# Range checks of a first unit's q, k and v: read again and squared near the end of the program, with a new order of all steps

## The chip, the core and the metric

One core of a Trainium2 chip runs the whole program. The metric is the device time of one execution in microseconds (us); lower is better. The engines are named as in the profile: PE (matmul), PEld (its weight loads), DVE (vector engine), ACT (scalar engine), POOL (GpSimd, which here issues most of the transfers) and SP (which issues the rest).

## What is computed

A gated linear recurrence over 768 positions for 4 batches and 8 heads of width 48, then a two-layer network on its output with squared ReLU:

```python
a_re_n, a_im_n = a_re * scale, a_im * scale   # scale = min(mag, 0.999) / (mag + 1e-6)
for t in range(S):
    S_re, S_im = ar * S_re - ai * S_im + k_t (x) v_t, ar * S_im + ai * S_re
    y[:, :, t] = q_t . S_re
x = y as (3072, 384)
h = x @ w_in                     # w_in (384, 2048), float64
out = maximum(h, 0)**2 @ w_out   # w_out (2048, 384), float64
```

Inputs q, k, v, a_re and a_im are float32.

## The kernel before

`fast_path` cuts the 3072 rows into six **units** of 512 rows (`NU`, numbered 0 to 5). For each unit `load(n)` brings a, q, k and v in, `chain(n)` turns the gates into running products (normalising, a scan over the positions, scaling of q and k), `pairs(n)` computes scores and sums per pair of heads on PE, and `dense(n, grp)` runs the two-layer network on the unit's rows, 256 at a time. The last unit has its own first layer (`whole`, L1922 to L1978) and every second layer from unit 1 on is done with seven products in place of eight (`seven`), its matmuls at L2051 in steps called `half`: eight matmuls each. Before any of that, the float64 weights are fetched in sixteen pieces and put into float32 by `convert`: two ACT operations (L975, L976) and two DVE operations (L978, L981) for each piece.

The fast path holds only for inputs in a certain range, so it also computes **checks**. `squares(j)` (called in `rest`, L1534 for q and k, L1537 for v) squares what a unit has loaded and sums it into `sums`; ACT does it, writing the squares to a scratch tile `junk`. For one unit this is six operations of 128x768. Near the end of the program `inspect(i)` reads each of the sixteen weight pieces a second time (a POOL transfer at L996 into a quarter of the tiles `ff`, of 768 KB), and DVE looks at their bits (`look`, L1001 and L1003). Piece i uses quarter i modulo 4, so the transfer of piece i waits for the look of piece i-4. When every check is done, `collect` (DVE, L2143 to L2156) puts them together, one PE matmul (L2160) adds over the partitions, and DVE (L2162) writes `flag`. Each engine then loads the flag into a register (L882) and branches on it (L2234, L2262): to `general_path`, a slow kernel for any input, or to the last steps of the fast path. These last steps, `plan.ends`, are what is left of the last `seven` after its matmuls are issued and isn't PE's: four DVE additions (L2074) that gather the results into the output tiles `ot`, and three transfers of output rows (L2002).

Two constants set what this change touches. `AFTER` is the number of units whose `squares` isn't run in `rest`, but by `squares_of`, after all `inspect` steps. It is 0 in the kernel before. `squares_of(n, j)` for j = 0, 1, 2 (q, k, v) issues a POOL transfer of the unit's q, k or v (768 KB, in runs of 768 bytes) into one quarter of `ff`, and one ACT operation of 128x1536 that squares it in place and sums into `sums`.

The order of the instructions on each engine is made by a planner (`Plan`). Every piece of work is a **step**, with an engine, a duration, what it reads and writes, and a number from the list `ORDER`, which has one entry for each step in the order in which the code creates them. The planner plays the program through: whenever an engine is free, it takes that one of its ready steps that has the smallest number. In the kernel before, the order that comes out is on every engine the ascending order of the numbers. An engine runs its queue strictly in this order, so a step whose inputs aren't there holds up all that stand behind it on the same engine. Where PE would stand still for long, the planner puts in matmuls on the identity whose result nobody reads (L880, "fill").

Names of steps in the prediction: the first transposes of unit 0's scaled q and k by PE are L1710, their copies out of PSUM by ACT are L1713, the scores are L1732, and the first layer of the network begins at L1850.

Of the kernel before, what the change touches and what calls it, by code (L numbers as in the profile page):

```python
# [767 lines left out]
def fast_path(ctx, tc, q, k, v, a_re, a_im, moe_w_in, moe_w_out, out, flag, ots, blocks_of):  # L768
# [69 lines left out]
    AFTER = 0  # L838
# [255 lines left out]
    def chain(n):  # L1094
# [503 lines left out]
        def rest(*zs):  # L1598
# [6 lines left out]
            for z in zs:  # L1605
                twist(z)
                if n >= AFTER:
                    squares(z)
# [660 lines left out]
```

## Time and profile before

| | us |
|---|---|
| median of 3 runs | 650.94 |
| lowest and highest of them | 650.93, 651.6 |
| the profiled execution, its own time | 652.71 |
| its span, first to last instruction | 651.0 |

The mean clock that PE was granted over the span is 0.997. The span is read as three parts: from the start to about 85 us, where unit 0 is prepared and its scores are computed and where all the fill lies; from there to about 648 us, where PE runs with hardly a gap; and the last 3 us, in which the last results are added and written out.

### The profile page before, as it was taken

How to read it: one execution, taken by the hardware profiler on the slowest of the kernel's cores; microseconds unless marked ns; L12 is line 12 of the kernel's file. 1: busy time of each engine (PE TensorE's matmuls, PEld its weight loads, DVE VectorE, ACT ScalarE, POOL GpSimd, SP SyncE). 2: the span in 40 equal slices, each digit the busy share in tenths (PEclk: the TensorE clock that was granted, in tenths of full speed). 3: DMA queues.
4: the chain of work that ended last, by engine and by line, in shares of the span. 5: the costliest groups of instructions: out<-in, count | busy, mean ns of one | idle time of the engine just before them, and what ended most of it. 6: DMA issues, size and time to landing. Idle time of an engine off the chain costs nothing.

```text
span 651.0 us, 13374 instructions
## 1 busy us (share of the span) xinstructions
PE 641.1 (98%) x5046; PEld 575.9 (88%) x5046; DVE 571.2 (88%) x1187; ACT 382.8 (59%) x652; POOL 152.4 (23%) x258
## 2 busy tenths in 40 slices
PE   8998999999999999999999999999999999999998
PEld 7988987578778988999988998989999989988997
DVE  7999999999799998988997996995979998359993
ACT  7989889956665265368166648156658164145500
POOL 6503455123200022051043051121050030022210
PEclk9998999999999999999999999999999999999999
DMA  7972679237620156352176354165260162257651
GB/s 224 298 255 57 163 213 203 72 89 189 165 82 2 37 126 149 93 143 52 49 161 146 73 131 88 24 152 159 58 171 16 45 143 66 61 202 242 209 184 31
DMA packets 34630, 81.79 MB, mean 126 GB/s; under 512 B 7894, under 2 KB 13411, under 8 KB 34556
## 3 DMA queue, kind: packets, MB, share of 16 engines
q0 software_dynamic: 17024, 58.60, 33.6%
q1 hardware_dynamic: 15356, 20.04, 12.1%
q10 hardware_dynamic: 2176, 2.20, 1.2%
q8 instruction: 42, 0.69, 0.5%
q14 instruction: 32, 0.26, 0.1%
HBM read 48.76 MB, written 4.72 MB: 82 GB/s over the span
## 4 chain that ended last, share of the span: by engine, by line
PE 73%; DVE 12%; ACT 4%; DMA 3%; issue 2%; SPq 0%; POOL 0%; DVEq 0%; ACTq 0%; POOLq 0%
PE d L1850 24%; PE d L2051 24%; PE d L1897 5%; PE sc L1732 5%; PE yp L1790 3%; PE tr L1762 2%; PE d L1943 2%; PE yp L1794 2%; PE tr L1943 2%; DVE f L1243 1%; PE sc L1943 1%; DMA aq<-in_a_im_dram 1%; PE d L1710 1%; DVE g L2065 1%; DVE aq L1228 1%
## 5 line engine op out<-in xcount | busy, mean ns | idle before, releaser
L1850 PE MATMUL d<-xT,w 128*128 128x256 f32 x912 | 203.2, 380 | 0.0
L1850 PEld LDWEIGHTS d<-xT,w 128*128 128x128 f32 x912 | 171.8, 190 | 24.0 <-issue 0.4
L2051 PE MATMUL d<-w,g 128*128 128x192 f32 x576 | 101.0, 327 | 0.0
L2051 PEld LDWEIGHTS d<-w,g 128*128 128x128 f32 x576 | 94.3, 190 | 1.2 <-issue 0.4
L1882 ACT ACTIVATE g<-d 128x512 f32<-128x512 f32 x76 | 45.0, 592 | 81.7 <-PE d L1850 79.0
L2051 PE MATMUL d<-T,g 128*128 128x192 f32 x432 | 77.1, 329 | 0.4 <-DVE g L2065 0.3
L2051 PEld LDWEIGHTS d<-T,g 128*128 128x128 f32 x432 | 70.6, 190 | 2.0 <-DVE g L2065 0.6
L2007 POOL DMA_DIRECT2D out_dram<-ot x22 | 12.5, 569 | 202.3 <-DVE ot L2074 181.3
L1682 ACT COPY QT<-aq 32x512 f32<-32x512 f32 x57 | 35.0, 615 | 39.7 <-DVE aq L1679 27.9
L1639 POOL DMA_DIRECT2D KC<-f x56 | 35.0, 630 | 80.8 <-DVE f L1593 30.3
L2065 DVE TENSOR_TENSOR g<-g 128x512 f32<-128x512 f32 x72 | 48.1, 685 | 4.8 <-PE d L2051 4.0
L1883 ACT ACTIVATE g<-g 128x512 f32<-128x512 f32 x80 | 50.5, 631 | 2.6
L1679 DVE STREAM_TRANSPOSE aq<-f 128x768 f32<-128x768 f32 x40 | 49.0, 1277 | 0.3
L1800 ACT COPY yt<-yp 112x512 f32<-112x512 f32 x24 | 26.5, 1106 | 34.2 <-PE yp L1794 34.2
L880 PEld LDWEIGHTS d<-ident 128*128 128x128 f32 x348 | 42.6, 203 | 3.0 <-POOL ident masks.py:199 1.7
L880 PE MATMUL d<-ident 128*128 128x128 f32 x348 | 43.3, 287 | 1.7 <-POOL ident masks.py:199 1.7
L1593 DVE TENSOR_TENSOR f<-aq 128x768 f32<-128x768 f32 (+1 forms) x56 | 44.0, 838 | 0.5
L1897 PE MATMUL d<-w,g 128*128 128x384 f32 x128 | 43.7, 491 | 0.0
L1732 PE MATMUL sc<-QT 96*64 96x128 f32 (+1 forms) x736 | 41.0, 258 | 1.5 <-ACT QT L1713 0.8
L1732 PEld LDWEIGHTS sc<-QT 96*64 96x64 f32 x736 | 37.1, 140 | 4.6 <-issue 2.3
L1738 DVE TENSOR_TENSOR A<-sc,mask 128x512 f32<-128x512 f32 x45 | 29.8, 681 | 9.2 <-PE sc L1732 9.2
L1897 PEld LDWEIGHTS d<-w,g 128*128 128x128 f32 x128 | 23.7, 190 | 15.0 <-issue 0.4
(276 smaller groups left out, 1167.5 us busy)
## 6 DMA issues: line engine op xcount, KB each, us to landing
QT<-aq SPq DMA_DIRECT2D x152, 64.0 KB
f<-in_moe_w_in_dram POOLq DMA_DIRECT2D x8, 768.0 KB, 6.0
f<-in_moe_w_out_dram POOLq DMA_DIRECT2D x8, 768.0 KB, 5.0
out_dram<-ot POOLq DMA_DIRECT2D x22, 192.0 KB, 2.8
KC<-f POOLq DMA_DIRECT2D x20, 192.0 KB, 4.5
xT<-yt SPq DMA_DIRECT2D x36, 96.0 KB
aq<-in_q_dram POOLq DMA_DIRECT2D x8, 384.0 KB, 5.4
aq<-in_k_dram POOLq DMA_DIRECT2D x8, 384.0 KB, 5.7
```

Source lines behind the costliest of these rows:

```text
L880: plan = Plan(lambda b: pe.matmul(bank[b][:, 0:C], lhsT=ident, rhs=ident, start=True, stop=True), ["d2", "d1", "d0"], lambda ap: tc.nc.val ...
L1593: lambda j=j, r=r, o=o: dve.tensor_tensor(out=o[:, :, :, r * D:(r + 1) * D], in0=qk[:, j], in1=a[:, r], op=ALU.mult), late[z])
L1639: lambda i=i, queue=queue, lo=lo, hi=hi, a0=a0, a1=a1: queue.dma_start(out=kc[lo:hi, i], in_=nat[a0:a1]),
L1679: lambda nat=nat, dst=dst, j=j: dve.transpose(out=dst[:, j], in_=nat), rank)
L1682: lambda b=b, t=t, T6=T6: act.copy(out=t[32 * b:32 * b + 32, b], in_=T6[32 * b:32 * b + 32, i % 2, b]),
L1732: pe.matmul(sa[r:r + C // 2, j, :, lo:32], lhsT=T[:, j, 1, h, ts(late, C // 2)], rhs=T[:, j, 0, h].rearrange("p (c t) -> p c t", c=W)[:, : ...
L1850: pe.matmul(ps, lhsT=w1[:, f // FP, m, ts(f % FP, C)], rhs=xT[:, n % 2, m, ts(grp, G)], start=(m == 0), stop=(m == NM - 1))
L1882: act.activation(out=o, in_=ps, func=AF.Relu)
L1883: act.activation(out=o, in_=o, func=AF.Square)
L1897: pe.matmul(ps, lhsT=gt[:, f % 2, ts(i, C)], rhs=w2[:, f], start=(f == 0), stop=(f == NF - 1))
L2051: pe.matmul(bank[b][:, 0:DH], lhsT=gs(r, h)[:, j - 4 * h], rhs=w(j), start=first and j == 0, stop=last and j == NT - 1)
L2065: step("DVE", tt(4 * C), gk(x0, h) + gk(x1, h), gk(o, h), lambda: dve.tensor_tensor(out=gs(o, h), in0=gs(x0, h), in1=gs(x1, h), op=op), (0 ...
```

## The change

The code differs in one constant, and in the numbers of `ORDER`:

```diff
-    AFTER = 0
+    AFTER = 1
```

With it `rest` leaves out six steps of unit 0, and the program gains six before `verdict`:

```python
if n >= AFTER:
    squares(z)
...
for n in range(AFTER):
    for j in range(3):
        squares_of(n, j)
verdict()
```

The number of steps stays the same (2434), so the old and the new list can be laid beside each other: the entries of the six left out are taken from the old list, and the six added stand ahead of the last three, which are `collect`, the matmul of the verdict and the flag. The last lines of the two lists:

```diff
-5840 5931 5855 5960 5901 6014 5933 6071 5947 6098 5976 6119 6030 6169 6088 6184 6114 6213
-6135 6227 6186 6245 6200 6275 6301 6356 6362
+5897 6013 5938 6058 5959 6072 5999 6126 6030 6163 6074 6180 6089 6220 6143 6237 6179 6264
+6197 6279 6236 6310 6253 6349 6365 6419 6426
```

Nearly every number differs, most of them little. Laid out by engine, the numbers say this of the places that the prediction uses:

| place | old numbers | new numbers |
|---|---|---|
| the six squares of unit 0 (ACT) | 259, 267, 288, 296, 484, 523 | left out |
| q, k and v of unit 0 near the end: transfers (POOL) | none | 6197, 6236, 6253 |
| their squares (ACT) | none | 6279, 6310, 6349 |
| first L1710 of unit 0 (PE) | 542 | 548 |
| one conversion, L975 and L976 (ACT) | 640, 649 | 500, 514 |
| one L1565 of 128x192 and one L1585 of unit 0 (DVE) | 547, 573 | 472, 521 |
| look of the last weight piece (DVE) | 6275 | 6264 |
| look of the piece before it (DVE) | 6245 | 6237 |
| the addition next to that look (DVE, L2074) | 6259 | 6234 |
| the half of eight matmuls that this addition waits for (PE) | 6239 | 6211 |
| PE steps with a number above that half's, without the verdict's | 14 | 17 |
| `collect` (DVE) | 6301 | 6365 |
| the last addition (DVE, L2074) that stands ahead of `collect` in the new order | 6356 | 6359 |
| the half that this addition waits for (PE) | 6317 | 6328 |
| PE steps with a number above that half's, without the verdict's | 8 | 8 |
| the verdict's matmul (PE) | 6356 | 6419 |
| PE steps behind it, eight matmuls each | 6359, 6372, 6385, 6398, 6411, 6424 | 6422, 6435 |
| the flag (DVE) | 6362 | 6426 |

The numbers are used as ranks only: they say what stands ahead of what on an engine.

256 rows, old and new, of the table ORDER are left out of this document.

## The prediction

> **What bounds the kernel now.** I read the page's busy times first, then the windows by stage.
>
> ```profile
> PE 641.1 (98%) x5046; PEld 575.9 (88%) x5046; DVE 571.2 (88%) x1187; ACT 382.8 (59%) x652; POOL 152.4 (23%) x258
> L880 PE MATMUL d<-ident 128*128 128x128 f32 x348 | 43.3, 287 | 1.7 <-POOL ident masks.py:199 1.7
> 28.00:42.00 14.00, 12.44 (x107) 11.77 (x104) 12.45 (x49) 12.06 (x18) 4.44 (x8) 1.00 1.02 324
> 42.00:58.40 16.40, 14.75 (x118) 13.39 (x117) 16.16 (x52) 16.23 (x25) 1.63 (x3) 1.00 0.26 79
> 58.40:84.90 26.50, 26.30 (x433) 24.30 (x433) 25.40 (x58) 20.86 (x31) 11.98 (x20) 0.94 0.60 140
> 84.90:160.00 75.10, 75.10 (x365) 57.28 (x366) 73.39 (x143) 60.65 (x100) 28.43 (x42) 1.00 0.64 153
> 160.00:576.00 416.00, 414.37 (x3445) 378.00 (x3440) 361.33 (x736) 223.92 (x395) 76.74 (x121) 1.00 0.39 96
> ```
>
> The columns of a window are its length, then the busy time of PE, PEld, DVE, ACT and POOL, the clock, the DMA share and GB/s. PE looks full everywhere, but 43.3 us of it is fill (L880), all ahead of 84.9. From 84.9 to 576 PE stands still for 416.00 - 414.37 = 1.6 us. So the program is a front of 85 us, in which PE waits for others, and then a block of PE work that nothing shortens here. The front can be won, or the end.
>
> In the front both DVE and ACT are full. From 42.00 to 58.40 ACT works 16.23 of 16.40 us and DVE 16.16. DVE's idle time from 28.00 to 84.90 is 1.55 + 0.24 + 1.10 = 2.9 us. The chain of waits goes through ACT just before PE's first scores:
>
> ```profile
> 49.13 0.92 ACT junk L1537 x2
> 53.15 0.82 ACT junk L1537 x2
> 53.97 1.84 ACT xT L976
> 56.50 1.91 ACT QT L1713 x4
> 58.46 3.60 PE sc L1732 x32
> 639.81 8.01 PE d L2051 x48
> 647.85 0.35 DVE ot L2074
> ```
>
> Here two of the checks that the change moves (L1537, squares of v) lie on the chain, ahead of the copies (L1713) that PE waits for. At the other end the chain is 48 matmuls and then one DVE addition.
>
> **The change, part one: what goes.** The six squares, by the groups of ACT from 24 to 58.4 us:
>
> ```profile
> L1534 ACT ACTIVATE junk<-aq 128x768 fp8e5<-128x768 f32 x4 | 3.4, 859 | 0.1
> L1537 ACT ACTIVATE junk<-v 128x768 fp8e5<-128x768 f32 x2 | 1.6, 824 | 0.0
> L1534 ACT ACTIVATION_READ_ACCUMULATOR junk<-aq 128x1 f32 x4 | 0.8, 189 | 0.0
> L1537 ACT ACTIVATION_READ_ACCUMULATOR junk<-v 128x1 f32 x2 | 0.4, 187 | 0.0
> L976 ACT ACTIVATE w<-w 128x768 f16<-128x768 int16 x4 | 7.8, 1944 | 0.1
> L975 ACT ACTIVATE w<-w 128x768 uint32<-128x768 uint32 x4 | 3.7, 936 | 0.0
> ```
>
> 3.4 + 1.6 + 0.8 + 0.4 = 6.2 us of ACT go. The new numbers put one conversion, L975 and L976, 0.94 + 1.94 = 2.9 us, ahead of the first copy L1713 in their place, so ACT has 6.2 - 2.9 = 3.3 us less ahead of it. On the chain itself stood 0.92 + 0.82 = 1.7 us.
>
> What is late next is DVE, which loses no instruction. The first transposes (L1710) read what DVE has multiplied, and DVE was without a gap there. The new numbers even put two more DVE operations ahead of them:
>
> ```profile
> 53.18 0.46 DVE L1585 TENSOR_TENSOR aq<-aq,e 128x288 f32<-128x288 f32 x1
> 53.56 0.35 DVE L1565 TENSOR_TENSOR f<-aq,e 128x192 f32<-128x192 f32 x1
> 84.84 1.13 PE L1850 MATMUL d<-xT,w 128*128 128x256 f32 x4
> 58.40:62.00 3.60, 3.54 (x33) 3.21 (x33) 3.60 (x10) 3.57 (x4) 1.58 (x3) 0.53 0.38 86
> ```
>
> That is 0.46 + 0.35 = 0.8 us later for the transposes, if nothing is gained, and 0 if DVE finds as much idle time ahead of them to fill. Both ends are near, and I take the middle: **the front ends 0.4 us later**. The bounds are wider. Below nothing: all of DVE's idle time is closed, -2.9 us. Above: the window from 58.40 shows PE at a clock of 0.53 for 3.6 us, which costs about 0.47 x 3.6 = 1.7 us; a second stretch like it, with the 0.8, makes +2.5 us.
>
> **Part two: what comes.** Three transfers of 768 KB on POOL and three squares of 128x1536 on ACT.
>
> ```profile
> L1114 ACT ACTIVATE f<-aq 128x1536 f32<-128x1536 f32 x10 | 14.9, 1489 | 3.6 <-DMA aq<-in_a_im_dram 3.5
> L1114 ACT ACTIVATION_READ_ACCUMULATOR f<-aq 128x1 f32 x10 | 1.9, 192 | 0.0
> DMA to landing us min/median/max: 4.6/5.4/9.5
> 620.00:651.00 31.00, 27.81 (x172) 27.25 (x170) 19.37 (x46) 1.58 (x3) 2.58 (x4) 1.00 0.29 99
> 628.43 0.56 DVE L1001 TENSOR_SCALAR f<-f 128x768 uint32<-128x768 uint32 x1
> 629.03 0.95 DVE L1003 TENSOR_REDUCE odd<-f 128x1 f32<-128x768 uint32 x1
> ```
>
> A square is 1.49 + 0.19 = 1.7 us. ACT is busy 1.58 of the last 31 us and POOL 2.58, so 5.1 us of squares and three issues cost nothing there: their cover is idle engines. The landing times are those of the same 768 KB at L996. What they could delay is the verdict. Let E be the end of PE's last matmul (647.82 before). A half of eight matmuls takes 8.01 / 6 = 1.335 us. The last of the three transfers needs the quarter of weight piece 14, and that piece's look stands behind an addition that waits for a half with 17 PE steps behind it: E - 22.8. With the addition (0.35) and the look (0.56 + 0.95) that is E - 20.9; landing after 5.4 to 9.5 us E - 15.5 to E - 11.4; squared by E - 9.7 at the latest. `collect` can't start much sooner anyway: the addition ahead of it waits for a half with 8 steps behind it, E - 10.8. So the third square is in time for PE's verdict.
>
> **Part three: where the verdict stands.** In the old order six halves stand behind the verdict's matmul on PE, in the new one two. These rows, from the timeline and, for the register load, from the tile `flag`, price that:
>
> ```profile
> 633.90 0.41 DVE L2143 TENSOR_SCALAR x<-sums 128x12 f32<-128x12 f32 x4
> 635.68 0.16 DVE L2156 TENSOR_REDUCE good<-good 128x1 f32<-128x7 f32 x1
> 639.62 0.19 PE L2160 MATMUL tr<-col,good 128*1 128x1 f32 x2
> 639.85 0.14 DVE L2162 TENSOR_SCALAR flag<-tr 1x1 int32<-1x1 f32 x1 [1.40 <-PE tr L2160]
> 642.65 0.35 DVE L2074 TENSOR_TENSOR ot<-ot,d 128x192 f32<-128x192 f32 x1 [2.65 <-PE d L2051]
> L882 DVEq TENSOR_LOAD <-flag x1: 539/539/539, 642.7 to 642.7; - x1
> 646.47 1.08 DVE L2074 TENSOR_TENSOR ot<-ot,d 128x192 f32<-128x192 f32 x3 [3.47 <-issue]
> 647.85 0.35 DVE L2074 TENSOR_TENSOR ot<-ot,d 128x192 f32<-128x192 f32 x1 [0.30 <-PE d L2051]
> ```
>
> `collect` takes 635.84 - 633.90 = 1.9 us, so it is done by E - 7.8 at the latest. The flag is written 639.99 - 639.62 = 0.37 us after the verdict's matmul starts. DVE loads it at 642.7, and its next operation, the first of the four behind the branch, starts at 646.47: **3.8 us from load to work**, of which "issue" says that it waited for nothing the profile shows. Before, this fitted under PE's last matmuls: three additions ran by 647.55, and the last one waited only for PE. In the new order the verdict's matmul starts at E - 2 x 1.335 - 0.1 = E - 2.8, the flag is there at E - 2.4, DVE goes on at E + 1.4, does three additions (1.08) and starts the last at E + 2.4. It was E + 0.03. The rest, the last transfer out, stays as it was behind that addition. **The end costs 2.4 us.** Bounds: 0, if the 3.8 us shrink to the 0.54 of the load; and +4.4, if the verdict also comes 2 us late.
>
> The Trainium skill, page "Advanced Engine Details and Errata", section "Control Flow Timing", gives a compare-and-branch about 108 ns, which speaks against this price: an estimate from that figure would leave the end at 0 and the sum at 0.4. The page "Runtime: NRT & Kernel Launch", section "Instruction fetch mechanics", says that a taken branch out of the window of fetched pages stalls for a fetch of its target. The row of 3.47 us agrees with the second.
>
> **Sum.** 0.4 + 2.4 = +2.8 us, on the profiled execution 652.71 + 2.8 = 655.5 (its span 651.0 + 2.8 = 653.8). The median of the runs shown lies 1.77 us under the profiled time, and I carry the difference over: 650.94 + 2.8 = **653.7 us**. 0.2% is 1.3 us, about what a measurement of this kernel tells from no change.
>
> **The rivals.**
>
> *ACT was the front's limit after all.* For it: the chain runs through ACT, from the squares to the copies and from them to PE's scores. Against it: DVE's 16.16 of 16.40. It decides if DVE's operations ahead of the transposes were themselves waiting for ACT in steps too short to see. Then all 2.9 us of idle time go: -2.9 + 2.4 = -0.5, 650.4 us, not slower. Chance 0.15.
>
> *The branch costs little.* For it: the row of 3.47 us is a single case, in which DVE was in no hurry. Against it: nothing in the profile names another cause. If DVE goes on right after its load of 0.54 us, it is at work by E - 1.8, the end costs 0, and the sum is 0.4: 651.3 us. Chance 0.1. With the first rival together, -2.9, 648.0 us: the only way to be clearly faster, with a chance of 0.1.
>
> *The checks come too late.* Runs of 768 bytes land later than the weights, or the looks, which stand earlier in the new order, wait for their pieces and hold DVE up. My margin from `collect`'s end to the verdict is 7.8 - 2.8 = 5 us; a third landing after over 14 us uses it up, and then the last two halves wait in PE's queue behind the verdict. With 2 us more: +4.8, 655.7 us. Chance 0.1.
>
> The forecast has 0.55: 653.7, its own range 651.9 (front -1.45, half of DVE's idle time) to 655.8 (front +2.5).
>
> **How the numbers follow.** Slower by over 0.2%, above 652.2: the forecast without its lower end, 0.52, and the late checks, 0.1, together 0.62. Within: that lower end, 0.03, the first rival, 0.15, and the cheap branch, 0.1, together 0.28. Faster: both rivals at once, 0.1. The range takes in the first rival and the late checks: 650.1 to 656.2.
>
> **What would show it.** Front: the start of the first L1850, 84.84 before, within -2.9 to +2.5; fill (L880) about 43 us. ACT busy less in the window to 58.4, DVE the same. End: 16 matmuls of L2051 behind L2160, a wait "issue" of some 3.5 us on DVE, and the last L2074 some 2.4 us behind PE's end in place of 0.03. I am wrong if the span behind the last matmul stays at 3.2 us, or if the first L1850 starts by 81.

## The result, and the profile after

| | before | after |
|---|---|---|
| median of the runs, us | 651.27 (4 runs) | 659.43 (4 runs) |
| profiled execution, us | 652.71 | 658.09 |
| its span, us | 651.0 | 656.4 |

The ratio is 1.0117, with a 95% interval of 1.0072 to 1.0161: slower by some 7.6 us. The forecast was 653.7 us, which is slower too, but the time lies outside its range of 650.1 to 656.2. So the sign was right and the size was not: two terms are to be looked for, one of them at the end, one that the forecast didn't have.

The profile after, first two lines of the page (busy times, and the group of filling matmuls):

```profile
PE 639.4 (97%) x5054; PEld 574.1 (87%) x5054; DVE 571.7 (87%) x1187; ACT 382.4 (58%) x646; POOL 155.9 (24%) x261
L880 PE MATMUL d<-ident 128*128 128x128 f32 x356 | 43.5, 283 | 1.6 <-POOL ident masks.py:199 1.6
```

ACT's busy time is what it was (382.8 before): what left the front came back at the end. The fill is the same too, 43.5 us against 43.3. Now the windows by stage (length, then the busy time of PE, PEld, DVE, ACT and POOL, the clock, the DMA share and GB/s), and the timeline of PE and DVE at the end:

```profile
42.00:58.40 16.40, 14.77 (x126) 14.10 (x125) 16.14 (x50) 16.27 (x20) 1.62 (x3) 1.00 0.23 68
58.40:84.90 26.50, 25.33 (x434) 22.90 (x433) 25.74 (x58) 20.92 (x32) 14.01 (x24) 1.00 0.70 163
84.90:95.00 10.10, 8.92 (x41) 7.57 (x41) 10.06 (x14) 8.70 (x12) 4.68 (x6) 1.00 0.57 142
95.00:160.00 65.00, 65.00 (x311) 48.70 (x311) 61.52 (x128) 48.31 (x84) 22.17 (x34) 1.00 0.56 142
160.00:360.00 200.00, 197.25 (x1610) 176.31 (x1608) 179.32 (x359) 114.92 (x203) 39.08 (x64) 1.00 0.40 101
360.00:576.00 216.00, 216.00 (x1844) 200.77 (x1838) 181.96 (x377) 109.73 (x195) 37.74 (x58) 1.00 0.38 92
sum 578.00, PE 571.27 PEld 510.45 DVE 514.55 ACT 338.50 POOL 130.64; mean PE 81.61 PEld 72.92 DVE 73.51 ACT 48.36 POOL 18.66
```

```profile
646.37 0.19 PE L2160 MATMUL tr<-col,good 128*1 128x1 f32 x2
646.49 2.87 PE L2051 MATMUL d<-T,QT 128*128 128x192 f32 x16
...
641.60 0.16 DVE L2156 TENSOR_REDUCE good<-good 128x1 f32<-128x7 f32 x1
646.59 0.15 DVE L2162 TENSOR_SCALAR flag<-tr 1x1 int32<-1x1 f32 x1 [2.37 <-PE tr L2160]
651.71 1.27 DVE L2074 TENSOR_TENSOR ot<-ot,d 128x192 f32<-128x192 f32 x4 [4.97 <-issue]
```

Two things stand there that the profile before did not have. PE stands still where it was full: 10.10 - 8.92 = 1.18 us just behind 84.9 us (before: none), and 2.75 us between 160 and 360 (before: 1.25). And at the end DVE does nothing for 4.97 us behind the flag, while PE's last matmul ends at 646.49 + 2.87 = 649.36: the last of the four additions starts at 651.71 + 1.27 - 0.35 = 652.63, 3.27 us behind PE's end. Before, it was 0.04.

A word on what to compare with. The profiled execution of before had the stretch of 3.6 us at a clock of 0.53 that the prediction shows; the one of after had none. The first experiment below keeps before's order up to the last products and its profiled execution has a clock of 1.00 up to 620 us, so PE's progress is read against that one.

### The profile page after: what moved, and what is told of

It is laid out like the page before. It is cut to its first block, busy times and chain, and to the rows that moved or that the text cites. A ratio compares the mean times of both kernels' runs of the same rounds, so it can differ in the third digit from the quotient of the medians.

```text
span 656.4 us, 13403 instructions
## 1 busy us (share of the span) xinstructions
PE 639.4 (97%) x5054; PEld 574.1 (87%) x5054; DVE 571.7 (87%) x1187; ACT 382.4 (58%) x646; POOL 155.9 (24%) x261
## 4 chain that ended last, share of the span: by engine, by line
PE 79%; ACT 6%; DVE 6%; DMA 4%; issue 2%; SPq 2%; POOL 0%; DVEq 0%; ACTq 0%
PE d L1850 27%; PE d L2051 26%; PE d L1897 5%; PE sc L1732 4%; PE yp L1790 3%; PE yp L1794 2%; PE tr L1762 2%; DMA QT<-aq 2%; PE d L1943 2%; SPq L1691 2%; PE tr L1943 2%; PE sc L1943 1%; PE tr L1305 1%; ACT T L976 1%; DMA xT<-yt 1%
## 5 line engine op out<-in xcount | busy, mean ns | idle before, releaser
L1850 PE MATMUL d<-xT,w 128*128 128x256 f32 x912 | 204.0, 380 | 0.0
L1850 PEld LDWEIGHTS d<-xT,w 128*128 128x128 f32 x912 | 171.8, 190 | 24.8 <-DVE ot L2074 0.3
L2051 PE MATMUL d<-w,g 128*128 128x192 f32 x576 | 100.2, 327 | 0.0
L2051 PEld LDWEIGHTS d<-w,g 128*128 128x128 f32 x576 | 94.4, 190 | 1.1 <-issue 0.4
L2051 PE MATMUL d<-T,g 128*128 128x192 f32 x432 | 77.5, 329 | 0.0
L2051 PEld LDWEIGHTS d<-T,g 128*128 128x128 f32 x432 | 70.6, 190 | 2.0 <-issue 0.8
L2007 POOL DMA_DIRECT2D out_dram<-ot x22 | 12.4, 566 | 217.1 <-DVE ot L2074 195.9
L880 PE MATMUL d<-ident 128*128 128x128 f32 x356 | 43.5, 283 | 1.6 <-POOL ident masks.py:199 1.6
L1732 PE MATMUL sc<-QT 96*64 96x128 f32 (+1 forms) x736 | 39.5, 252 | 2.7 <-DMA QT<-aq 2.7
L1732 PEld LDWEIGHTS sc<-QT 96*64 96x64 f32 x736 | 35.6, 137 | 6.3 <-issue 3.1
```

Source lines behind the costliest of these rows:

```text
L880: plan = Plan(lambda b: pe.matmul(bank[b][:, 0:C], lhsT=ident, rhs=ident, start=True, stop=True), ["d2", "d1", "d0"], lambda ap: tc.nc.val ...
L1732: pe.matmul(sa[r:r + C // 2, j, :, lo:32], lhsT=T[:, j, 1, h, ts(late, C // 2)], rhs=T[:, j, 0, h].rearrange("p (c t) -> p c t", c=W)[:, : ...
L1850: pe.matmul(ps, lhsT=w1[:, f // FP, m, ts(f % FP, C)], rhs=xT[:, n % 2, m, ts(grp, G)], start=(m == 0), stop=(m == NM - 1))
L2051: pe.matmul(bank[b][:, 0:DH], lhsT=gs(r, h)[:, j - 4 * h], rhs=w(j), start=first and j == 0, stop=last and j == NT - 1)
```

## The experiments

Each was timed in five rounds beside the kernel before on the same chip; the ratios are to that kernel. The verdict's matmul is L2160, a half is eight matmuls of L2051 (1.3 us).

### The verdict alone, moved

```diff
-""".split()]
+""".split()]; ORDER[2432], ORDER[2433] = 6410, 6418
```

> The kernel before with one thing of the change alone: the verdict's matmul stands behind four more halves of the last products on PE (2 behind it instead of 6), as after the change; squares, transfers and the rest of the order as before. Theory of the prediction: PE ends where it ended and the last addition comes 2.4 us later, ratio 1.0037. Theory from the two traces: the same mechanism at the size seen after the change, last addition 3.2 us and the end 3.9 us later, ratio 1.0060. Rival (the late end came from the late squares and transfers, not from the verdict's place): no change, ratio 1.000.

Measured: 654.48 us, ratio 1.0052 (1.0035 to 1.0069). Its timeline at the end, and the register loads of the flag in the view of that tile:

```profile
643.23 0.19 PE L2160 MATMUL tr<-col,good 128*1 128x1 f32 x2
643.35 2.87 PE L2051 MATMUL d<-T,QT 128*128 128x192 f32 x16
...
643.46 0.14 DVE L2162 TENSOR_SCALAR flag<-tr 1x1 int32<-1x1 f32 x1 [2.37 <-PE tr L2160]
648.58 1.27 DVE L2074 TENSOR_TENSOR ot<-ot,d 128x192 f32<-128x192 f32 x4 [4.97 <-issue]
```

```profile
L882 DVEq TENSOR_LOAD <-flag x1: 542/542/542, 643.6 to 643.6; - x1
L882 PEldq TENSOR_LOAD <-flag x1: 497/497/497, 643.6 to 643.6; - x1
```

PE ends at 646.22, the last addition starts at 649.50: 3.28 us behind, as after the change. So the verdict's place alone makes the tail, with no late square or transfer in the program. From load to work DVE needs 648.58 - 643.6 = 4.9 us, where it needed 3.8 before.

### The verdict back, in the changed kernel

```diff
-        step("DVE", 3.4, [], [("good",), ("x",)], collect, (LATE, 99), after=checked)
+        step("DVE", 0.2, [], [("good",), ("x",)], collect, (LATE, 99), after=checked)
...
+""".split()]; ORDER[2432], ORDER[2433] = 6366, 6380
```

> The changed kernel with the verdict's matmul three halves earlier on PE (5 behind it instead of 2; the planner is given 0.2 us for the collecting step instead of 3.4) and the flag ahead of one addition; squares, transfers and all other places as after the change. If the verdict's place makes the tail, the end comes 3.2 to 3.9 us earlier than in the changed kernel, ratio to the kernel before about 1.005 instead of 1.0117, and PE still ends 1.5 us later than before. Rival (late squares and transfers make the tail): ratio stays 1.0117. Rival (the collecting step really isn't done that early): PE waits at the verdict and the gain is under 1 us.

Measured: 655.19 us, ratio 1.0063 (1.004 to 1.0085). The timeline at the end:

```profile
642.80 0.19 PE L2160 MATMUL tr<-col,good 128*1 128x1 f32 x2
646.93 2.76 PE L2051 MATMUL d<-T,QT 128*128 128x192 f32 x16
...
644.53 0.35 DVE L2074 TENSOR_TENSOR ot<-ot,d 128x192 f32<-128x192 f32 x1 [1.35 <-PE d L2051]
648.17 1.08 DVE L2074 TENSOR_TENSOR ot<-ot,d 128x192 f32<-128x192 f32 x3 [3.29 <-issue]
649.73 0.35 DVE L2074 TENSOR_TENSOR ot<-ot,d 128x192 f32<-128x192 f32 x1 [0.48 <-PE d L2051]
```

The last addition waits for PE again (0.48 <- PE) and stands 0.04 us behind its end, so with five halves behind the verdict the tail is gone: 0.0054 of the ratio, 3.5 us. The two intervals just overlap; that it is the tail which went is read from these rows. In the changed kernel `collect` had been done 4.6 us ahead of the verdict (641.76 against 646.37): the verdict's number puts it behind all but two halves, and the planner reckons 3.4 us for a `collect` that takes 1.95. But 1.0063 is left, and PE's last matmul starts at 649.37, against 645.89 in the run above. That part is not the tail.

### No checks at all

```diff
-                check("ACT", ac(Y), [(("qk", "k")[r], j)], [], lambda r=r: act.activation(
+                check("ACT", ac(Y), [(("qk", "k")[r], j)], [], lambda r=r: n and act.activation(
...
-            check("ACT", ac(Y), [("v", vs(n))], [], lambda: act.activation(
+            check("ACT", ac(Y), [("v", vs(n))], [], lambda: n and act.activation(
```

The planner still counts the six squares of unit 0, but they are not issued, so every engine keeps its order.

> The kernel before without the first unit's six squares at all (the range checks of its q, k and v are left out), order and tail as before: what the freed ScalarE alone is worth. Theory that VectorE takes over at once: ratio 0.9995 to 1.000. Theory that ScalarE limited the front by the 1.7 us of squares on the chain: ratio 0.9974. Rival (ScalarE is the limit for all 6.2 us): under 0.995.

Measured: 651.03 us, ratio 0.999 (0.9971 to 1.001): nothing that can be told from none. Its windows beside those of the run with the late verdict (the sum is over all windows from 42 to 620 us; the last row is the first L1850 of unit 0; first this run, then that one):

```profile
58.40:84.90 26.50, 25.50 (x421) 23.22 (x418) 26.12 (x59) 21.26 (x32) 11.81 (x20) 1.00 0.65 158
sum 578.00, PE 574.41 PEld 512.28 DVE 515.97 ACT 344.17 POOL 128.98; mean PE 82.06 PEld 73.18 DVE 73.71 ACT 49.17 POOL 18.43
82.94 1.13 PE L1850 MATMUL d<-xT,w 128*128 128x256 f32 x4
```

```profile
58.40:84.90 26.50, 26.08 (x438) 23.67 (x439) 26.12 (x59) 21.75 (x32) 11.61 (x20) 1.00 0.65 156
84.90:95.00 10.10, 10.10 (x48) 8.91 (x47) 10.06 (x12) 9.94 (x15) 6.77 (x11) 1.00 0.77 229
160.00:360.00 200.00, 198.94 (x1666) 178.12 (x1662) 181.77 (x361) 115.08 (x203) 38.22 (x63) 1.00 0.41 103
360.00:576.00 216.00, 215.61 (x1766) 199.74 (x1766) 180.38 (x378) 108.65 (x195) 39.11 (x61) 1.00 0.37 90
sum 578.00, PE 574.43 PEld 512.33 DVE 516.71 ACT 346.21 POOL 129.46; mean PE 82.06 PEld 73.19 DVE 73.82 ACT 49.46 POOL 18.49
83.71 1.13 PE L1850 MATMUL d<-xT,w 128*128 128x256 f32 x4
```

PE is busy for 574.41 us here and 574.43 there, and DVE works 26.12 of 26.50 us in the last part of the front in both. But the front itself does move: PE begins the first layer at 82.94 us here and at 83.71 there, 0.77 us earlier in the same order (82.72 to 83.05 in the four runs below that leave the squares out and keep the old order). In this execution the lead is lost again near 345 us: from the start of one group of scores (L1732) to the next step, L1762, PE takes 2.41 us, and 1.33 with the late verdict. The profiled execution of before takes 2.30 us there, with all its squares, so it isn't their doing. ACT's 6.2 us buy PE some 0.7 to 1.0 us in the front, less than the times can tell.

### The move in the old order

Here the six squares go as above, and the three loads and squares come at the end (`squares_of` for one unit), while all else keeps its order and the verdict its six halves:

```diff
-    for n in range(AFTER):
+    for n in range(1):
...
+""".split()]; ORDER[2431:2431] = [6214, 6285, 6250, 6316, 6264, 6347]; ORDER[2437] = 6349
```

> The move alone, without the new order: the first unit's six squares are left out of their old place, loaded again and squared near the end as in the change, while every engine keeps the order of the kernel before, the verdict with 6 halves behind it. Theory from the traces (the move itself frees ACT and the new order loses the time): front 0.5 to 1.1 us earlier, tail as before, ratio 0.9985 to 0.9995. Prediction's view (VectorE takes over in the front at once): front within 0.4 us of before, ratio 1.000. Rival (the checks come too late for the verdict's old place): PE waits for the third square and the collecting step, 1.5 to 4 us, ratio 1.0025 to 1.006.

Measured: 658.47 us, ratio 1.0111 (1.0092 to 1.0131), about twice what the rival allowed. The wait for the branch is not to blame, the last addition stands 0.04 us behind PE's end. That end is 651.26, against 646.22 with the late verdict: 5.0 us later. ACT's timeline, PE's with the window around it, and the DMA queues from 653 us on (packets, MB, share):

```profile
636.77 1.48 ACT L1020 ACTIVATE f<-f 128x1536 f32<-128x1536 f32 x1 [1.08 <-DMA f<-in_v_dram]
638.16 0.19 ACT L1020 ACTIVATION_READ_ACCUMULATOR f<-f 128x1 f32 x1
638.25 0.30 ACT L2069 COPY ot<-d 128x192 f32<-128x192 f32 x1
```

```profile
638.60 4.54 PE L2051 MATMUL d<-w,QT 128*128 128x192 f32 x16 [4.00 <-ACT ot L2069]
638.60:643.10 4.50, 4.50 (x18) 4.06 (x18) 1.95 (x11) 0.00 (x0) 0.00 (x0) 0.62 0.09 25
```

```profile
q10 hardware_dynamic: 9, 0.01, 1.2%
```

So PE waits 4.0 us for one copy, and the wait costs more than itself: the 16 matmuls behind it take 4.54 us, where 16 of them take 2.76 elsewhere, at a mean clock of 0.62. Together that is 5.8 us; the end is only 5.0 us later because PE had come to the last products 0.9 us earlier (one addition, L2074, starts at 616.00 us here and at 616.90 with the late verdict). Another 2 us stand behind the last addition (656.6 - 651.30 = 5.3 us to the end of the span, 3.15 before): nine packets, a sixteenth of ACT's last output transfer, move only after 653 us, when nothing else does. What held them is not shown.

I took it that a copy of a finished bank (L2069) stands behind the third square on ACT, and the square behind the load of v. So the next two runs put the copy ahead of the third square, one with the verdict where the changed kernel has it, one with four halves behind it:

```diff
+""".split()]; ORDER[2431:2431] = [6214, 6285, 6250, 6316, 6264, 6347]; ORDER[2437] = 6349; LATER = {2436: [2374]}; ORDER[2438], ORDER[2439] = 6410, 6418
```

`LATER` gives a step more steps to wait for in the planner (2436 is the third square, 2374 the copy); the second of the runs has 6373, 6374 at the end. Both have the 0.2 us for `collect` too, as do all the runs below.

> The move in the old order, with the tail of the changed kernel: six squares gone from their place, loads and squares near the end, the copy of ScalarE now ahead of the third square, the verdict with 2 halves behind it on PE. It differs from the changed kernel only by the new order of the rest. If the new order costs PE 3.1 us and the verdict's place 3.4 us, then ratio 1.005 and PE ends where it ends in the run without the squares (last matmul near 646.0 us). Rival (the late transfers and squares slow PE or the tail by themselves): ratio 1.010 to 1.0117.

> As the run before it, but with the verdict earlier, 4 halves behind it on PE, as soon as the third square and the collecting step allow. If the move by itself costs nothing but the late verdict: PE ends near 646.0 us, the flag stands some 4 us before that, the last addition comes within 1 us of PE's end, ratio 0.999 to 1.002. Rival (the third square is too late even here): PE waits at the verdict, ratio over 1.004. A ratio under 0.998 would mean a version that beats the kernel before.

Measured: 658.92 us, ratio 1.0116 (1.0077 to 1.0155), and 656.62 us, ratio 1.0073 (1.0051 to 1.0095). Neither came out as my theory had it; the first lies where its rival put it. PE still waited 3.3 and 3.4 us for the copy, and the 16 matmuls behind each wait took 4.55 and 4.43 us. The timeline of the second (POOL's and ACT's rows) and its outputs' view (L2007) say why:

```profile
627.29 0.89 POOL L1016 DMA_DIRECT2D f<-in_v_dram  x1 [0.25 <-DVE ot L2074]
628.18 0.75 POOL L2007 DMA_DIRECT2D out_dram<-ot  x1
...
637.18 0.32 ACT L2069 COPY ot<-d 128x192 f32<-128x192 f32 x1 [1.84 <-DMA out_dram<-ot]
```

```profile
DMA to landing us min/median/max: 2.1/2.9/8.6
```

The copy no longer waits for a square. It waits for the tile it writes into, which an output transfer is still reading, and that transfer was issued on POOL's queue behind the load of v: 8.6 us to land, where the median of the 22 is 2.9. So the next run puts both output transfers ahead of the second and third load, and the copy ahead of the second square:

```diff
-            rank, m * 3072 * 2, dur=0.74, group=n)
+            rank, 1, lat=0.2, dur=0.74, group=n)
...
+LATER = {2433: [2361, 2363], 2435: [2361, 2363], 2434: [2374], 2436: [2374]}; ORDER[2438], ORDER[2439] = 6390, 6391
```

> The move in the old order again, with the two output transfers of POOL put ahead of the second and the third late load instead of between them, ScalarE's copy into the output tile ahead of the second and the third square, and the verdict with 3 halves behind it. If the late loads cost by standing ahead of the output transfers (PE waited 3.3 to 4.0 us for a copy into a tile that one of them was still reading), that wait goes, PE ends near 646 us, and the late flag leaves 0.5 to 2 us: ratio 1.000 to 1.003. Rival (the third square is too late by itself): PE waits at the verdict for over 1 us and the ratio stays over 1.004.

Measured: 653.38 us, ratio 1.0029 (1.0007 to 1.005). PE's wait for the copy is gone. PE's end is 646.93, 0.71 us later than with the late verdict, and the last addition stands 0.97 us behind it, with three halves behind the verdict: 0.71 + 0.93 = 1.6 us of the 1.9 that the ratio means. (Its profiled execution, 654.82 us, has the late packets of an output transfer too, and lies 1.4 us over its median.) So the loads near the end are not hidden by themselves: PE waited 3.3 to 4.0 us, and lost 1.7 to 1.8 more behind the wait, where they stood ahead of an output transfer on the same queue; where they stood behind it, PE's end came 0.7 us later. The changed kernel's new order avoids that; its third square and `collect` are in time.

### The new order of the rest

What is left of the changed kernel, 1.0063, must then be its new order. Three tiles matter here: ACT copies a unit's result into yt, SP's transfers bring yt into xT, which the first layer (L1850) reads, and QT holds the q and k that the scores (L1732) read. PE's busy time from 42 to 620 us is 571.27 us against 574.43 with the late verdict, 3.16 us less, and its last matmul starts 649.03 - 645.89 = 3.14 us later: about the same number from two sides. By the windows above, 0.75 us of it is lost from 58.4 to 84.9 us, 1.18 from 84.9 to 95, 1.69 from 160 to 360, and 0.39 is won behind 360. The second of these, in the timeline of the changed kernel (PE's, POOL's and ACT's rows) and then of the run with the late verdict (POOL's and ACT's):

```profile
91.76 0.45 PE L1850 MATMUL sc<-xT,w 128*128 128x256 f32 x1 [1.18 <-DMA xT<-yt]
...
82.56 0.72 POOL L962 DMA_DIRECT2D xT<-in_moe_w_out_dram  x1 [5.15 <-DVE w L981]
83.28 3.33 POOL L1091 DMA_DIRECT2D v<-in_v_dram  x4
...
82.89 1.47 ACT L1114 ACTIVATE f<-aq 128x1536 f32<-128x1536 f32 x1
84.35 1.11 ACT L1800 COPY yt<-yp 112x512 f32<-112x512 f32 x1
```

```profile
87.17 0.72 POOL L962 DMA_DIRECT2D xT<-in_moe_w_out_dram  x1 [5.20 <-ACT f L1222]
87.88 0.90 POOL L1091 DMA_DIRECT2D v<-in_v_dram  x1
...
83.82 1.12 ACT L1800 COPY yt<-yp 112x512 f32<-112x512 f32 x1 [1.53 <-PE yp L1794]
84.74 1.48 ACT L1114 ACTIVATE f<-aq 128x1536 f32<-128x1536 f32 x1
```

In the new order a piece of w_out, 768 KB, and four loads of v go out 4.6 us earlier, ahead of the last two transfers of xT (SP issues them at 85.5 and 86.1), and PE waits for those. On ACT the square of the next unit (L1114) stands ahead of the last copy into yt, where the old order has it behind: the copy starts 0.5 us later, and SP's two transfers with it. Two runs take the collision of the transfers away, in the changed kernel with the early verdict; neither moves L1114. The first puts fetch (149) and loads behind the small copy `gate` (339), which waits until xT has landed:

```diff
+LATER = {k: [339] for k in (149, 868, 870, 871, 872)}
```

> The changed kernel with the early verdict (ratio 1.0063), and on POOL's queue one fetch of a 768 KB piece of w_out and the four loads of the second unit's v put behind the small copy that waits for the last transfers of xT, instead of ahead of it; a few later steps change places by that. If these transfers delay xT, PE's wait for xT (2.0 us in the run with the early verdict) goes, and PE ends 1.2 to 2 us earlier: ratio 1.003 to 1.0045. If the later wait for QT near 176 us is only a consequence of it, it goes too and the ratio is 1.001 to 1.003. Rival (xT is late for another reason, or the loads are missed later): ratio stays 1.0063 or rises.

The second puts a tiny copy ahead of them that waits for ACT's last copy into yt, so that they go out just behind SP's transfers:

```diff
-                pairs(n, (2 * z, 2 * z + 1))
+                pairs(n, (2 * z, 2 * z + 1)); z and step("POOL", 0.2, [("yt", 1)], [("gate", 5)], lambda: pool.tensor_copy(out=gate[0:1, 0:1], in_=yts[1][0:1, 0:1]), (CONV, 0))
...
+ORDER[339:339] = [856]; LATER = {k: [339] for k in (149, 869, 871, 872, 873)}
```

> The changed kernel with the early verdict (ratio 1.0063), and one tiny copy on POOL that waits for ScalarE's last copy into yt, put ahead of the 768 KB fetch of w_out and the four v loads: POOL then issues them just behind SP's last transfers of xT, 1 to 3 us later than before, and not behind their landing as in the run with the gate first. If the order of these issues is what costs the 1.5 us at xT, PE's wait for xT falls from 2.0 to under 0.5 us, without the new wait at 122 us that the gate brought; PE ends 1 to 2 us earlier and the ratio is 1.0035 to 1.005. Rival (the transfers collide all the same, being 1 us apart): the wait stays over 1 us and the ratio at 1.006.

Measured: 655.70 us, ratio 1.0058 (1.0027 to 1.0088), and 655.21 us, ratio 1.0063 (1.0043 to 1.0083). Neither is faster than the run with the early verdict. Yet the wait itself did go; windows and timeline of the first:

```profile
84.90:95.00 10.10, 10.10 (x48) 8.88 (x48) 10.07 (x14) 9.35 (x13) 6.13 (x4) 1.00 0.16 28
95.00:160.00 65.00, 63.07 (x291) 46.28 (x290) 59.06 (x125) 45.63 (x79) 25.11 (x38) 0.97 0.64 150
```

```profile
121.98 0.55 PE L1305 MATMUL tr<-ident,xn 128*128 128x128 f32 x3 [1.93 <-ACT xn L1502]
```

PE is full up to 95 us and loses the same 1.93 us at 122 us, and some clock with it: the next unit's loads, which had to wait too, are late for its chain. In the second run PE waited 0.2 us at its first L1850 instead of 2.0 for xT, but 1.1 us at 169 us for one of ACT's copies into yt. Its profiled execution is the fastest of its twelve (653.53 us), and there PE ended 1.2 us earlier than in the run with the early verdict; the medians show none of it. So the transfers that go out early do make xT late, but taking them away gained nothing that the time shows.

Two last runs divide the program at 95 us: in each list, the numbers under 950 come from the other order.

> The reverse: new order for the first 95 us, then the old order with the tail of the run that has the output transfers ahead of the late loads (ratio 1.0029 there). If the front of the new order costs 2.0 us and the freed ScalarE gives the old front 0.8 us that is lost again later, PE ends 1.5 to 2.5 us later than there and the ratio is 1.005 to 1.0065. Rival (the loss sits behind 95 us): ratio within 0.001 of 1.0029.

> The changed kernel with the early verdict (ratio 1.0063), but for the first 95 us every engine keeps the order of the kernel before (without the six squares); from there on the new order. If the new order costs PE 2.0 us in the front (to 92 us) and about 1.2 us later, PE ends 2 us or more earlier than in the run with the early verdict, and the ratio is 1.002 to 1.0035. Rival (the loss sits behind 95 us): ratio 1.005 to 1.0065.

Measured: new order in front 655.79 us, ratio 1.0051 (1.0033 to 1.0069), against 1.0029 for the same tail with the old one: 0.0022, 1.4 us, though the intervals overlap. In the traces PE is 1.6 us later at 636 us. Old order in front: 654.85 us, ratio 1.0041 (1.0024 to 1.0057). That seemed to say that front and rest share the loss, but in this run PE did 38 filling matmuls at 80 to 87 us where the kernel before does 16, a work of the planner's own. So I took 22 away:

```diff
-                    self.fill[n] = max(0, int((stop - lost) / self.EACH)), spare[0]
+                    self.fill[n] = min(4 if free[e] > 70 else 999, max(0, int((stop - lost) / self.EACH))), spare[0]
```

> The run with the old order for the first 95 us and the new one behind it, with one thing mended: there the planner had put 38 filling matmuls where the kernel before has 16 (30 of them at 83.6 us, while PE waited for nothing); now 16. If those 22 matmuls of 0.116 us stood on PE's path, PE ends 2.5 us earlier than in that run, near 646.5 us, and the ratio falls from 1.0041 to 1.000 to 1.002; then the new order costs its 2 us in the front and under 1 us behind it. Rival (they only covered a wait for xT, or the new order behind 95 us costs over 1 us): ratio 1.0025 to 1.004.

Measured: 655.85 us, ratio 1.0064 (1.0037 to 1.009). The rival had it: where the fill had been, PE now waited.

```profile
PE d L1850 <- issue: 1.8, 1, 1.8
```

With the squares gone, the old numbers don't make the old order: ACT took a square of the next unit (L1114) ahead of a copy into yt, as in the changed kernel, and the transfers of xT began 1.6 us later than with the late verdict. So this run says nothing clean about the part behind 95 us, and which step of the new order makes PE wait for QT between 160 and 360 us (2.7 us in two waits, 0.4 in the run with the late verdict) stays open. The second of the two, 1.06 us at 349 us, isn't in the run with the early verdict, whose order is the same there, and stands near the scores where before's own profiled execution lost 1.0 us. No run here was clearly faster than the kernel before.

## Why the prediction was wrong

*The verdict's place: right, and too small.* The step read: 3.8 us from load to work, so the last addition at E + 2.4. It came at E + 3.27. The flag was where I had it (written by 646.74, E - 2.6, forecast E - 2.4). The term that was off is the 3.8 us. How long DVE is away, and where the last addition starts behind PE's end E, by the halves behind the verdict (from the timelines and the register loads of each run):

| halves behind | run | load to work, us | last addition behind E, us |
|---|---|---|---|
| 6 | before | 3.81 | 0.04 |
| 5 | verdict back | 3.63 | 0.04 |
| 4 | move in the old order, second | 3.88 | 0.04 |
| 3 | outputs ahead of the loads | 3.85 | 0.97 |
| 2 | after | 4.93 | 3.27 |
| 2 | verdict alone | 4.94 | 3.28 |
| 2 | move in the old order, first | 4.59 | 2.93 |

With two halves behind it, PE has already issued its last matmul when the flag is there (in the other runs it loads the flag some 2.7 us before its last matmul starts), so all five engines load the flag at once and branch together. In the three runs where that happens DVE needs 4.59 to 4.94 us; in the eleven where PE branches 0.8 us or more after DVE, 3.56 to 4.02. I had priced a branch with PE by one without it. The DMA view between DVE's load and its first instruction behind the branch, for the changed kernel (646.8 to 651.6 us) and then for the kernel before (642.7 to 646.3 us):

```profile
q14 instruction: 4, 0.03, 2.4%
q8 instruction: 1, 0.02, 1.7%
```

```profile
q14 instruction: 4, 0.03, 3.2%
```

These are all the packets that moved in that time: instructions, fetched while DVE did nothing. The packet on q8, of 16 KB, comes 1.6 to 2.1 us behind PE's own load of the flag in every run. That DVE waits for these packets, and that PE's is what makes it wait longer, fits all runs but is not shown. DVE's own record of the branch (L2234) is 0.07 us long; the price is the 2.8 us or more of nothing behind it. The page "Runtime: NRT & Kernel Launch" of the Trainium skill, section "Instruction fetch mechanics", which says that a taken branch out of the fetched window stalls, agrees with all fourteen runs; it gives no price, and the 108 ns of the page "Advanced Engine Details and Errata", section "Control Flow Timing", is not what the branch costs here.

*The rest behind the last addition: not quite as it stood.* 656.4 - 652.63 = 3.77 us against 651.0 - 647.85 = 3.15 before: 0.6 us more. With the verdict alone moved it is 653.2 - 649.50 = 3.70, so it comes with the verdict's place: the three runs with two halves have 3.7 to 4.0 us, the others 3.1 to 3.5, but for four with late packets.

*The front: near in size, but not by the mechanism.* The forecast was 0.4 us later, with DVE taking over at once. With the squares gone and the old order kept, PE begins the first layer 0.7 to 1.0 us earlier (82.72 to 83.05 us in five runs, against 83.71 with the late verdict), so ACT did hold the front back a little; the rival's 2.9 us would be a ratio of 0.9955, outside the 0.9971 to 1.001 measured without the squares. The new order takes this back and more: the first L1850 starts at 83.77 to 85.78 us in the five runs that have its front, and in the changed kernel PE's busy time is 0.75 us behind that run's by 84.9 us. One sign failed too: ACT is not less busy up to 58.4 us (16.27 us against 16.23), as the new order fills it again.

*"A block of PE work that nothing shortens": the step that failed.* I ended the front at 85 us and took what follows as given, since PE was full there. It was full because that order fed it. The change had its order found anew in all of the program, and I weighed only the steps that it moved around the squares and the verdict. The term stood at nothing in the sum, and it measured 3.1 us at PE's end: waits for xT (1.55 us) and QT (2.74 us), less what the run with the late verdict waits for itself. The order of the first 95 us made some 1.4 us of it in the one run that tried it alone, with intervals that overlap. Which steps of the new order make the rest is open. A block without gaps can't get shorter, but it can get longer; the new order's issues on POOL against SP's transfers at 82 to 86 us could have been compared before any run.

*The transfers near the end: right for the changed kernel only.* The third square was done at 639.0 (E - 10.4, forecast E - 9.7 at the latest) and `collect` at 641.76 (E - 7.6, forecast E - 7.8). "The checks come too late" is a real danger all the same: in the old order PE waited 3.3 to 4.0 us, by an output transfer behind a load and not by a late landing of the last load.

*The sum.* I carried over 1.77 us between the profiled time and the median as if profiling cost it. The profiled execution of before held two delays of its own: its stretch at a clock of 0.53 made the first L1850 1.13 us later than in the run with the late verdict, of the same order, and it lost another 1.0 us near 345 us. PE ended 1.59 us sooner in that run, and there the profiled time lies 0.4 us over the median.

So of the 7.6 us, about 3.5 are the verdict's place, and the rest, about 4.1, is the new order, against 2.4 and 0.4 forecast. The traces show 3.1 of these 4.1; the difference lies within the intervals.

## What to carry to other kernels

A full engine in the profile is full in the order that fed it: when a planner's whole list changes, compare the order of transfers queue by queue over all of the program, as a load that goes out 5 us earlier can delay one that an engine waits for. A verdict with a branch belongs where the busiest engine still has work for longer than the branch takes (here four halves, some 5.3 us); in the changed kernel it stood past that point, though what it waits for had been ready for 4.6 us. Loads that nothing waits for were nearly free here only behind the transfers that something waits for.

## What the hardware showed that I had not expected

- From the register load of the flag to the first instruction behind the branch: 3.56 to 4.02 us on DVE when PE branches later, 4.59 to 4.94 us when all five engines branch together. In the changed kernel and the kernel before, the DMA engines move only instructions in that time.
- Behind waits of 3.3 to 4.0 us, 16 matmuls of PE took 4.43 to 4.55 us in place of 2.76, at a clock of 0.62 to 0.64.
- A transfer of 192 KB on POOL's queue, issued just behind a load of 768 KB, landed in 8.6 us, where the median is 2.9; with the two output transfers ahead of the second and third load they landed in 3.6 and 4.9.
- The last sixteenth of an output transfer (9 of 144 packets) came 1.3 to 2.1 us behind the rest in four of the fourteen profiled executions, at the very end of the span, by nothing the trace shows.
- 6.2 us less work on an engine that was busy 99% of a stage (ACT, 16.23 of 16.40 us) moved the stage behind it by 0.7 to 1.0 us, and the program's time by nothing that can be told.
